# Transposes of x in 64-row halves among the query projections, the early weight bits in new places, and the first key exponential ahead of the denominator

## The chip, the core and the metric

The kernel runs on one core of one Trainium2 chip. The metric is the device time of one execution in microseconds (us), as the median of several runs. TensorE (PE) multiplies matrices and also does the transposes; VectorE (DVE), ScalarE (ACT) and GpSimd (POOL) do elementwise work, and SyncE (SP) issues the DMA transfers. Each engine works through its own instructions in program order, and engines wait for one another through semaphores.

## The reference, cut to what matters

```python
def phi(x):
    proj = np.einsum('bhsd,df->bhsf', x, w_phi)
    proj = proj - np.max(np.abs(proj), axis=-1, keepdims=True)
    return np.concatenate([np.exp(proj), np.exp(-proj)], axis=-1)
q_p, k_p = phi(q), phi(k)             # 8 batches, 8 heads, 576 tokens, 64 -> 2*128
kv  = np.einsum('bhsf,bhsd->bhfd', k_p, v)
z   = np.sum(k_p, axis=2)
num = np.einsum('bhsf,bhfd->bhsd', q_p, kv)
den = np.einsum('bhsf,bhf->bhs', q_p, z)[..., None] + 1e-06
x   = (num / den).transpose(0, 2, 1, 3).reshape(4608, 512)
h   = x @ w_in                         # 512 -> 2048
g   = h * np.tanh(softplus(h))
out = g @ w_out                        # 2048 -> 512
```

## The kernel before, in words

The program has two stages on one core: the attention, up to about 270 us of the trace, and the feed-forward layer after it. The change is in the attention and in the weight preparation that runs beside it.

The attention is cut into 36 units of 512 rows (`NU`). For a unit of keys there are these steps, named by their functions. `k_proj` (L292 in `project`) multiplies 64-row slices of the keys by `w_phi` into a PSUM tile `pp_k`: eight matmuls, the two 64-row halves of the partitions in turn. `k_center` takes the maximum `m_k` (L300) and subtracts it into `e_k` (L301), both on DVE. `k_exp` takes the two exponentials on ACT (L345 and L346). `k_sum` multiplies by the values into `kvps` (L309), and `k_store` copies `kvps` to `kv` on ACT (L371).

For a unit of queries: `q_proj` into `pp_q` (L292), `q_center` into `m_q` and `e_q` on DVE, `q_turn` transposes `e_q` into two tiles `dt` (L396; sixteen transposes of 64 rows), `q_exp` takes four exponentials of `dt` on ACT (L401), and `q_num` multiplies by `kv` into `num` (L309, two tiles). `q_den` copies the denominators from `num` to `r` on ACT (L421); `q_norm` takes the reciprocal and multiplies into `x` on DVE (L426, L429). A unit later `q_out` transposes x on PE into one tile `xt` (L438, four transposes of 128 rows), and `q_store` copies it to `xs` on ACT (L445) and sends it to `x_spill` by DMA (L446). In a middle unit PE runs in the order `dt`, `pp_k`, `xt`, `pp_q`, `num`, `kvps`, each step for another unit of rows.

PSUM tiles come from two pools. `ps_a` has two buffers, which `pp_k` and `pp_q` take in turn, so every `pp_q` of the middle units has the same buffer as the `pp_q` before it. `ps_b` has four buffers, shared by `dt`, `xt`, `num` and `kvps`. A tile's first write waits for the last reader of the tile that held the buffer before.

Beside this, `weight_ops` prepares 16 of the weight pieces in the attention (`EARLY`), one in about two units: `absolute` on ACT (L183), `clamp` (L186), `shift` (L190), `sign` (L194) and `scale` (L200) on DVE, then `low_scale` (L209), multiplications and sums on POOL, a cast on ACT (L243) and a subtraction on POOL (L247).

Near the end of the attention, `x_load` (L462) brings x back from DRAM and `x_block` casts it into blocks `xc` (L484), which go to `xc_spill` (L488).

The order on each engine is written out by hand: every step is registered with a planned time (`at(time, fn)`), the events are sorted by that time, and the sorted order is the program's order on each engine. The planned time has no other use; nothing waits for a clock. A unit is planned as 7.341 us (`STEP`), and `K_AT` and `Q_AT` are the offsets of its steps.

Of the kernel before, what the change touches and what calls it, by code (L numbers as in the profile page):

```python
# [8 lines left out]
F32 = mybir.dt.float32  # L9
# [7 lines left out]
P = 128  # L17
# [14 lines left out]
LEAD = 4  # L32
# [12 lines left out]
Q_AT = (1.52, 3.149, 6.11, 6.455, 1.875, 3.0, 6.564, 9.042)  # L45
T_AT = (0.95, 2.19, 4.9, 5.3, 8.55, 10.92, 12.6, 13.1)
JOIN = 0.99
JOIN_AT = ((-4.6, -4.5, -4.46, -3.7), (0.0, 0.9, 1.8, 2.8))
PRE = (11.72, 6.53)
CONV = (13.41, 14.719)  # L50
WORD_AT = 4.79
X0_AT = (38.06, 20.0)
X0_SUM_AT = 31.75
X0_BLOCK_AT = (26.35, 26.3, 22.18, 22.17, 22.16, 17.38, 17.33)
# [30 lines left out]
def attention_then_mish(ctx, tc, qT, kT, va, w_phi, w_in, w_out, w_out2, out):  # L85
# [80 lines left out]

    def weight_ops(kind, fp, k, quiet):

# [16 lines left out]
        def clamp():  # L185
            nc.vector.tensor_scalar(w(), w(), LARGE, SMALL, op0=ALU.min, op1=ALU.max)  # L186

# [23 lines left out]
        def low():  # L211
            if not quiet:
                low_scale()
            f, t = low_word(), piece[key][2]
            nc.gpsimd.tensor_tensor(t, f, t, op=ALU.mult)
# [54 lines left out]

        ops = [(0.0, absolute), (0.9, clamp), (1.35, shift), (1.8, sign), (2.5, scale)]
        if quiet:
            ops.insert(1, (0.2, low_scale))
# [8 lines left out]
    def project(raw, name, cuts=(0, 4)):  # L282

        parts = []
        for a, b in zip(cuts, cuts[1:]):
            ps = ps_a.tile([P, 2, 4, F], F32, tag="pp", name=f"pp_{name}_{a}")
# [6 lines left out]
        return parts  # L293

    def center(parts, name):
# [44 lines left out]

    def k_exp(n):
        e = k_live[n]
        for a, b in zip(cuts_of(n), cuts_of(n)[1:]):
            cols = slice(a * P, b * P)
            nc.scalar.activation(e[:, :, 1, cols], e[:, :, 0, cols], AF.Exp)  # L345
            nc.scalar.activation(e[:, :, 0, cols], e[:, :, 0, cols], AF.Exp, scale=-1.0)  # L346
# [33 lines left out]
    def q_proj(n):  # L380
        q_live[n] = project(q_live.pop(n), f"q_{n}")

    def q_center(n):
# [57 lines left out]
    def q_store(n):  # L441
        c, g = divmod(n, 2)
        ps = out_live.pop(n)
        xs = att.tile([P, 2, CH], F32, tag="xs", name=f"xs_{n}", bufs=2)
        nc.scalar.copy(xs, ps)  # L445
        nc.sync.dma_start(x_spill[c][:, 2 * g:2 * g + 2, :], xs)  # L446
# [30 lines left out]
    def x_block(s, b):  # L477
# [8 lines left out]
        xc[s].append(blk)  # L486
        if not seen_before[s] and s + 1 != seg2:
            nc.sync.dma_start(xc_spill[segs[s][0], b], blk.rearrange("p h k s -> p h (k s)").bitcast(F32))  # L488

# [290 lines left out]
    for u in range(NU):  # L780
# [5 lines left out]
        at(t + (LOAD_AT[1] if u > LEAD else V_AT[u]), v_load, u)  # L786
        at(t + a[0], k_proj, u)
        at(t + a[1], k_center, u)
        at(t + a[2], k_exp, u)
        at(after + a[3], k_sum, u)  # L790
# [9 lines left out]
        at(t + LOAD_AT[2] - early, q_load, u)  # L800
        at(t + a[0] - early, q_proj, u)
        at(t + a[1] - early, q_center, u)
# [6 lines left out]
        at(end + a[5] + 0.05, q_norm, u)  # L809
        at(close_by + a[6] + (1.78 if u in (NU - LEAD - 2, NU - LEAD - 1) else 0.0), q_out, u)  # L810
        at(close_by + a[7] + (0.9 if u == NU - 1 else 0.0), q_store, u)

# [33 lines left out]
    for i, pc in enumerate(pieces):  # L846
# [5 lines left out]
        else:  # L852
            clock = CONV[0] + CONV[1] * i - WORD_AT
            load_at = clock + WORD_AT + (LOAD_AT[3] if i else -12.0)
        at(load_at, weight_load, *pc)
        bits, sums, high, spill = weight_ops(*pc, quiet)
        for delay, op in bits:
            wait = base(2 * i + 1) + Q_AT[1] + 0.02 if i < 2 and delay else 0.0
            at(max(clock + delay * (0.85 if quiet else 1.0), wait - (0.49 if i == 0 else 0.0)), op)
        clock += LOW_AT[which] if quiet else WORD_AT  # L860
        for j, (cost, op) in enumerate(sums):
            at(clock, op)
            if pc[1] >= 2 and j in (high, len(sums) - 1):
                at(clock + SPILL_AT[j > high and not quiet], spill, int(j > high))
            clock += cost
            if i == EARLY - 1 and sums[j + 1:j + 2] and j + 1 == high:
                clock += 1.2

    for s, (sc, fps) in enumerate(segs):
# [10 lines left out]
        for i in range(4):  # L880
            at((begin - X0_SUM_AT if s == 0 else t_of(n - 2) + X_SUM_AT if late_sums else t + XS_AT[1] + (XS2 if s == 3 else 0.0)) + XS_AT[2] * i, x_sum, s, i)
        for b in range(7):
            if n >= AHEAD + 2:
# [144 lines left out]
```

## Time and profile before

| | us |
|---|---|
| median of 3 runs | 1017.37 (1017.09 to 1017.58) |
| profiled execution, its own time | 1015.56 |
| its span in the trace | 1013.7 |
| PE busy | 1004.0 (99%) |
| DVE busy | 759.9 (75%) |
| ACT busy | 505.1 (50%) |
| POOL busy | 277.2 (27%) |

The span runs from the first to the last recorded instruction; 1.86 us of the profiled execution lie outside it. The granted clock of TensorE was 1.0, the higher level of 2.4 GHz, in every stretch of the attention that is shown below. A row of a timeline gives the start and the length of one instruction, or of several of one kind, and, in brackets, how long the engine stood idle before it and what ended that. Matmuls are pipelined, so that the start of the next step tells more than the length of one. The records of one fp32 matmul are two, so x16 stands for eight matmuls.

### The profile page before, as it was taken

The page shows a single profiled execution, that of the slowest core. Times are in us where ns is not written, and L with a number is a line of the kernel's source. Part 1 is how long each engine was busy: PE and PEld are TensorE (multiplying, and loading weights), DVE is VectorE, ACT ScalarE, POOL GpSimd, SP SyncE. Part 2 cuts the span into 40 slices and gives each one's busy share as a digit, 9 for nine tenths or more (in the row PEclk, how much of TensorE's full clock was granted, in tenths as well). Part 3 has the DMA queues.
Part 4 walks back from the last instruction along what each step waited for, and adds up shares of the span by engine and source line. Part 5 has one row for each costly group of instructions (what it writes and reads, how often), then busy time and mean ns, then how long its engine had stood idle before and what let it go on. Part 6 is the DMA issues. An engine that isn't in the chain of part 4 may idle for free.

```text
span 1013.7 us, 28698 instructions
## 1 busy us (share of the span) xinstructions
PE 1004.0 (99%) x12298; PEld 956.9 (94%) x12298; DVE 759.9 (75%) x1184; ACT 505.1 (50%) x874; POOL 277.2 (27%) x251
## 2 busy tenths in 40 slices
PE   8999999999999999999999999999999999999998
PEld 7899999999899999999999999999999999999998
DVE  6899999999657788878985675757575757575755
ACT  5778777877754445554453433333333333333332
POOL 0454435545515244466436010101010101010101
PEclk9999999999999999999999999999999999999999
DMA  7556567776887869898858995858586858686841
GB/s 222 173 186 182 183 207 255 252 243 196 278 303 297 324 253 325 271 330 303 281 200 298 344 360 209 324 209 321 210 320 217 313 218 312 219 311 222 308 167 73
DMA packets 111199, 259.00 MB, mean 256 GB/s; under 512 B 8672, under 2 KB 47328, under 8 KB 109024
## 3 DMA queue, kind: packets, MB, share of 16 engines
q1 hardware_dynamic: 111072, 257.17, 71.9%
q8 instruction: 97, 1.59, 0.6%
q14 instruction: 30, 0.25, 0.1%
HBM read 179.27 MB, written 77.86 MB: 254 GB/s over the span
## 4 chain that ended last, share of the span: by engine, by line
PE 96%; ACT 2%; DVE 1%; DMA 1%; issue 0%; DVEq 0%; ACTq 0%
PE h L519 36%; PE o L671 22%; PE o L648 15%; PE num L309 6%; PE kvps L309 6%; PE pp_k L292 3%; PE pp_q L292 3%; PE dt L396 2%; PE xt L438 2%; ACT e_q L401 1%; DMA x_spill<-xs 1%; DVE e_k L301 0%; DVE m_k L300 0%; DMA head<-w_phi 0%; ACT e_k L345 0%
## 5 line engine op out<-in xcount | busy, mean ns | idle before, releaser
L519 PE MATMUL h<-xc,win 128*128 128x256 f32 x3024 | 380.4, 283 | 0.0
L519 PEld LDWEIGHTS h<-xc,win 128*128 128x128 f32 x3024 | 373.8, 192 | 4.5
L743 POOL TENSOR_TENSOR part<-part,du 128x512 f32<-128x512 f32 x18 | 23.3, 1297 | 425.7 <-DVE du L733 425.7
L671 PE MATMUL o<-wa,gh 128*128 128x256 f32 x720 | 130.7, 283 | 0.0
L671 PEld LDWEIGHTS o<-wa,gh 128*128 128x128 f32 x720 | 111.8, 192 | 0.0
L648 PE MATMUL o<-wout,gh 128*128 128x512 f32 x432 | 108.2, 392 | 0.0
L551 DVE TENSOR_TENSOR u<-h,u 128x512 f32<-128x512 f32 x72 | 49.4, 687 | 70.4 <-PE h L519 70.4
L671 PE MATMUL o<-wa,gl 128*128 128x256 f32 x360 | 100.7, 283 | 0.0
L671 PE MATMUL o<-wb,held 128*128 128x256 f32 x795 | 95.8, 281 | 0.2 <-DVE du L733 0.2
L671 PEld LDWEIGHTS o<-wb,held 128*128 128x128 f32 x795 | 94.9, 189 | 0.4 <-DVE du L733 0.4
L648 PEld LDWEIGHTS o<-wout,gh 128*128 128x128 f32 x432 | 77.7, 189 | 13.9
L309 PE MATMUL num<-kv,e_q 128*64 128x65 f32 x2304 | 78.5, 223 | 1.3 <-ACT e_q L401 0.8
L309 PEld LDWEIGHTS num<-kv,e_q 128*64 128x64 f32 x2304 | 72.2, 137 | 7.1 <-ACT e_q L401 2.3
L567 ACT ACTIVATE sb<-h 128x256 f32<-128x256 f32 x45 | 17.3, 385 | 120.0 <-PE h L519 85.8
L309 PE MATMUL kvps<-v,e_k 128*64 128x65 f32 (+1 forms) x2560 | 76.8, 222 | 0.0
L401 ACT ACTIVATE e_q<-dt 128x512 f32<-128x512 f32 x144 | 74.2, 604 | 4.3 <-PE dt L396 3.7
L570 ACT ACTIVATE u<-u 128x768 f32<-128x768 f32 x45 | 38.1, 846 | 72.8 <-DVE u L551 72.8
L309 PEld LDWEIGHTS kvps<-v,e_k 128*64 128x64 f32 (+1 forms) x2560 | 72.5, 137 | 1.7 <-issue 0.2
L606 ACT CAST gh<-sb 128x1024 fp32r<-128x1024 f32 x45 | 47.2, 1050 | 50.0 <-DVE sb L599 50.0
L671 PEld LDWEIGHTS o<-wa,gl 128*128 128x128 f32 x360 | 68.6, 192 | 0.0
L618 DVE TENSOR_TENSOR gl<-sb,gh 128x1024 fp32r<-128x1024 f32 x45 | 61.0, 1356 | 0.7 <-ACT gh L606 0.7
L648 PE MATMUL o<-wout,gl 128*128 128x512 f32 x216 | 57.7, 389 | 0.0
(101 smaller groups left out, 1592.2 us busy)
## 6 DMA issues: line engine op xcount, KB each, us to landing
win<-in_spill SPq DMA_DIRECT2D x44, 896.0 KB, 8.0
xc<-xc_spill SPq DMA_DIRECT2D x63, 512.0 KB, 5.8
xc_spill<-xc SPq DMA_DIRECT2D x56, 512.0 KB, 6.0
wa<-out_spill SPq DMA_DIRECT2D x29, 768.0 KB, 5.7
in_spill<-wst_in SPq DMA_DIRECT2D x24, 448.0 KB, 2.7
v<-va SPq DMA_DIRECT2D x32, 325.0 KB, 3.9
qraw<-qT SPq DMA_DIRECT2D x36, 256.0 KB, 3.7
x_spill<-xs SPq DMA_DIRECT2D x36, 256.0 KB, 2.9
```

Of the source, the lines that this page charges most:

```text
L292: nc.tensor.matmul(ps[:, j, n], src, w_phi2[rows], start=True, stop=True)
L309: nc.tensor.matmul(ps[rows], lhsT[:, rows], rhs[h], start=start, stop=stop, skip_group_check=True)
L396: nc.tensor.transpose(turned[n, h][:, jj, i], e[rows, jj, 0, i * P:(i + 1) * P], ident[rows, rows])
L401: nc.scalar.activation(e[:, s, h], ps, AF.Exp, scale=2.0 * s - 1.0)
L519: nc.tensor.matmul(ps, w, x, start=(i in (0, 2) and m == 0), stop=(m == 5), skip_group_check=True)
L551: nc.vector.tensor_tensor(u[:, 0:3:2] if second(n) else u[:, 1:3], hy, u2.unsqueeze(1).broadcast_to([P, 2, CH]), op=ALU.add)
L570: nc.scalar.activation(u[:, 0:3], u[:, 0:3], AF.Mish)
L606: nc.scalar.copy(gh, u_live[n][4])
L618: nc.vector.tensor_tensor(gl, u_live[n][4], g_live[n]["h"].bitcast(F32), op=ALU.subtract)
L648: nc.tensor.matmul(o_live[s][tt], g[:, 2 * f + which, cols], wout[fp][:, f, k], start=(first and g is gh and f == k == 0), stop=(last and ...
L671: nc.tensor.matmul(ps, g, w, start=(start and k == 0), stop=(stop and k == 2), skip_group_check=True)
L743: nc.gpsimd.tensor_tensor(cross, cross, d_live[s, tau][0].unsqueeze(1).broadcast_to([P, 2, CH]), op=ALU.add)
```

## The change

It has these parts.

- x's transposes. For units 3 to 32 of the queries, the new `q_proj_out` writes the eight projections of the unit and, among them, the transposes of x of the unit three before, as eight transposes of 64 rows into two tiles `xt0` and `xt1`. `q_store` copies the two tiles to `xs` in two instructions. Units 30 to 35 of x keep `q_out`.
- The early weight bits of pieces 2 to 15. The clamp goes from DVE to POOL. `absolute` and `clamp` stand one unit earlier; `shift` and `sign` stand on DVE between the keys' centring and the reciprocal; `scale` follows a unit later, again behind the keys' centring. `low_scale` is a step of its own.
- The first of a key unit's two exponentials goes ahead of the two `r` on ACT, the second stays behind them.
- The two parts of the projection of key unit 0 share one PSUM tile, `k_proj` of unit 5 comes 1.7 planned us earlier, the stores of the first seven `xc` blocks are steps of their own (`block_store`), and one `q_store` is 0.68 earlier.

```diff
+EXP_AT = 2.95
+BEAT_AT = (-5.73, -5.54, 1.9, 1.91, 9.24, 7.84)
+BEAT_LOW, BEAT_HI = 9.34, 16.43
+X0_STORE_AT = (16.4, 16.35, 16.3, 16.25, 16.2, 15.0, 14.9)
...
         def clamp():
-            nc.vector.tensor_scalar(w(), w(), LARGE, SMALL, op0=ALU.min, op1=ALU.max)
+            (nc.vector if quiet else nc.gpsimd).tensor_scalar(w(), w(), LARGE, SMALL, op0=ALU.min, op1=ALU.max)
...
         ops = [(0.0, absolute), (0.9, clamp), (1.35, shift), (1.8, sign), (2.5, scale)]
+        if early:
+            ops = list(zip(BEAT_AT, (absolute, clamp, shift, sign, scale, low_scale)))
+        elif not quiet:
+            ops = [(0.0, absolute), (0.6, clamp), (1.95, shift), (2.25, sign), (2.7, scale)]
...
+    def project_turn(raw, name, x, ps_x):
+
+        ps = ps_a.tile([P, 2, 4, F], F32, tag="pp", name=f"pp_{name}")
+
+        def proj(j, n):
+            rows = slice(j * D, (j + 1) * D)
+            nc.tensor.matmul(ps[:, j, n], raw[rows, n * P:(n + 1) * P], w_phi2[rows], start=True, stop=True)
+
+        def turn(h):
+            rows = slice(h * D, (h + 1) * D)
+            for i in range(2):
+                for t in range(2):
+                    nc.tensor.transpose(ps_x[h][:, i, t], x[rows, i, t], ident[rows, rows])
+
+        proj(1, 0)
+        turn(0)
+        for n in range(4):
+            proj(0, n)
+            if n < 3:
+                proj(1, n + 1)
+        turn(1)
+        return [(0, 4, ps)]
...
-    def k_exp(n):
+    def k_exp(n, s):
+        e = k_live[n]
+        nc.scalar.activation(e[:, :, s], e[:, :, 0], AF.Exp, scale=2.0 * s - 1.0)
...
+    def q_proj_out(n, m):
+        ps = [ps_b.tile([P, 2, 2, D], F32, tag="b", name=f"xt{h}_{m}") for h in range(2)]
+        q_live[n] = project_turn(q_live.pop(n), f"q_{n}", x_live.pop(m), ps)
+        out_live[m] = ps
...
-        nc.scalar.copy(xs, ps)
+        if isinstance(ps, list):
+            halves_of = xs.rearrange("p i (t h d) -> p h i t d", t=2, h=2)
+            for h in range(2):
+                nc.scalar.copy(halves_of[:, h], ps[h])
+        else:
+            nc.scalar.copy(xs, ps)
...
-        at(t + a[2], k_exp, u)
+        if u < LEAD:
+            at(t + a[2], k_exps, u)
+        else:
+            at(t + EXP_AT, k_exp, u, 1)
+            at(t + a[2], k_exp, u, 0)
...
-        at(t + a[0] - early, q_proj, u)
+        if 3 <= u <= NU - LEAD:
+            at(t + a[0], q_proj_out, u, u - 3)
+        else:
+            at(t + a[0] - early, q_proj, u)
```

On PE, in a middle unit of before, the four whole transposes of x (`xt`) stand between the projections of the keys and of the queries; `dt` is the transposed `e_q`.

```order
L396 MATMUL dt_16_2960<-ident,e_q_2799 128x64
L292 MATMUL pp_k_0_2977<-head,kraw_2805 128x128 x8
L438 MATMUL xt_2992<-ident,x_2864 128x128 x4
L292 MATMUL pp_q_0_3002<-head,qraw_2810 128x128 x8
L309 MATMUL num_16_3015<-kv_2062,e_q_2799 64x65 x8
```

In the same place after the change, the transposes are two blocks of four, one of each 64-row half, within the projections of the queries.

```order
L436 MATMUL dt_16_3061<-ident,e_q_2891 128x64
L300 MATMUL pp_k_3078<-head,kraw_2896 128x128 x8
L309 MATMUL pp_q_3095<-head,qraw_2900 128x128
L315 MATMUL xt_15_3093<-ident,x_2962 128x64 x4
L309 MATMUL pp_q_3095<-head,qraw_2900 128x128 x7
L315 MATMUL xt_15_3094<-ident,x_2962 128x64 x4
L340 MATMUL num_16_3120<-kv_2122,e_q_2891 64x65 x8
```

So `pp_q` now comes straight behind `pp_k`, and the last block of transposes straight ahead of `num`.

On DVE, one unit of before with weight work has the clamp and the shift ahead of the reciprocal of `r`, and the sign and the scale (`t_in`) behind the queries' centring (`m_q`, `e_q`).

```order
L300 TENSOR_REDUCE m_k_2900<-pp_k_0_2830 128x8
L301 TENSOR_TENSOR e_k_2899<-pp_k_0_2830,m_k_2900 128x2x512
L186 TENSOR_SCALAR w_in_0_2859<-w_in_0_2859 128x512
L190 TENSOR_SCALAR w_in_0_2859<-w_in_0_2859 128x512
L426 RECIPROCAL r_2905<-r_2905 128x8
L429 TENSOR_TENSOR x_2864<-num_15_2865,r_2905 128x256
L429 TENSOR_TENSOR x_2864<-num_15_2866,r_2905 128x256
L300 TENSOR_REDUCE m_q_2945<-pp_q_0_2850 128x8
L301 TENSOR_TENSOR e_q_2944<-pp_q_0_2850,m_q_2945 128x2x512
L194 SCALAR_TENSOR_TENSOR w_in_0_2859<-words_in_0_2697,w_in_0_2859 128x512
L200 TENSOR_SCALAR t_in_0_2953<-w_in_0_2859 128x512
```

After the change the shift and the sign stand there, the scale follows in the next unit, and nothing stands between `e_q` and the next unit's `m_k`.

```order
L331 TENSOR_REDUCE m_k_3155<-pp_k_3078 128x8
L332 TENSOR_TENSOR e_k_3154<-pp_k_3078,m_k_3155 128x2x512
L194 TENSOR_SCALAR w_in_1_2955<-w_in_1_2955 128x512
L198 SCALAR_TENSOR_TENSOR w_in_1_2955<-words_in_1_2842,w_in_1_2955 128x512
L466 RECIPROCAL r_3164<-r_3164 128x8
L469 TENSOR_TENSOR x_3119<-num_16_3120,r_3164 128x256
L469 TENSOR_TENSOR x_3119<-num_16_3121,r_3164 128x256
L331 TENSOR_REDUCE m_q_3212<-pp_q_3095 128x8
L332 TENSOR_TENSOR e_q_3211<-pp_q_3095,m_q_3212 128x2x512
L331 TENSOR_REDUCE m_k_3319<-pp_k_3241 128x8
L332 TENSOR_TENSOR e_k_3318<-pp_k_3241,m_k_3319 128x2x512
L204 TENSOR_SCALAR t_in_1_3322<-w_in_1_2955 128x512
```

On ACT after the change, a unit with a cast of weights has the two half copies of x, the cast and the first key exponential ahead of the two `r`; before, the order there was one copy, the two `r`, and both exponentials.

```order
L441 ACTIVATE e_q_2891<-dt_16_3061 128x2x4x64 x2
L488 COPY xs_3112<-xt_15_3093 128x4x64
L488 COPY xs_3112<-xt_15_3094 128x4x64
L247 CAST wst_in_0_3116<-w_in_0_2643 128x896
L374 ACTIVATE e_k_3154<-e_k_3154 128x2x512
L461 ACTIVATE r_3164<-num_16_3120 128x4
L461 ACTIVATE r_3164<-num_16_3121 128x4
```

The two `r` have thus moved behind a key exponential and, in such a unit, behind the cast.

## Rows read from the trace of the kernel before

**Rows 1.** Page, its head and part 1: busy time of the engines, share, instructions.

```profile
span 1013.7 us, 28698 instructions
...
PE 1004.0 (99%) x12298; PEld 956.9 (94%) x12298; DVE 759.9 (75%) x1184; ACT 505.1 (50%) x874; POOL 277.2 (27%) x251
```

**Rows 2.** Busy time by stretch: first units, 25 middle units, tail of the attention.

```profile
core 0: us, PE busy (x) PEld busy (x) DVE busy (x) ACT busy (x) POOL busy (x), PEclk, DMA share, GB/s
16.05:58.31 42.26, 41.17 (x1045) 37.77 (x1041) 37.55 (x47) 31.84 (x57) 17.48 (x17) 1.00 0.62 189
58.31:239.38 181.07, 181.07 (x4677) 168.34 (x4676) 166.79 (x226) 142.77 (x272) 84.65 (x79) 1.00 0.66 215
239.38:272.00 32.62, 31.32 (x741) 28.49 (x741) 24.66 (x38) 25.69 (x59) 19.88 (x16) 1.00 0.74 237
```

**Rows 3.** Timeline of PE in a middle unit.

```profile
157.57 0.71 PE L396 MATMUL dt<-ident,e_q 64*128 64x64 f32 x16
158.12 1.11 PE L292 MATMUL pp_k<-head,kraw 64*128 64x128 f32 x16
159.16 0.66 PE L438 MATMUL xt<-ident,x 128*128 128x128 f32 x4
159.74 1.16 PE L292 MATMUL pp_q<-head,qraw 64*128 64x128 f32 x16
160.83 2.09 PE L309 MATMUL num<-kv,e_q 128*64 128x65 f32 x64
```

**Rows 4.** Timeline of DVE in that unit.

```profile
158.25 1.23 DVE L301 TENSOR_TENSOR e_q<-pp_q,m_q 128x1024 f32<-128x1024 f32 x1
159.39 0.68 DVE L194 SCALAR_TENSOR_TENSOR w_in<-words_in,w_in 128x512 uint32<-128x512 uint32 x1
...
161.77 1.23 DVE L301 TENSOR_TENSOR e_k<-pp_k,m_k 128x1024 f32<-128x1024 f32 x1
163.17 0.20 DVE L426 RECIPROCAL r<-r 128x8 f32<-128x8 f32 x1 [0.18 <-ACT r L421]
...
165.40 1.22 DVE L301 TENSOR_TENSOR e_q<-pp_q,m_q 128x1024 f32<-128x1024 f32 x1
```

**Rows 5.** Timelines of DVE and PE early on, where `pp_q` waited for `e_q`.

```profile
49.21 1.22 DVE L301 TENSOR_TENSOR e_q<-pp_q,m_q 128x1024 f32<-128x1024 f32 x1
...
50.49 0.71 PE L292 MATMUL pp_q<-head,qraw 64*128 64x128 f32 x8
```

**Rows 6.** Timeline of PE, 0.04 us where `num` begins behind `pp_q`.

```profile
240.27 0.28 PE L292 MATMUL pp_q<-head,qraw 64*128 64x128 f32 x2
240.47 0.28 PE L309 MATMUL num<-kv,e_q 128*64 128x65 f32 x2
```

**Rows 7.** Timeline of ACT in the unit of rows 3.

```profile
158.35 2.07 ACT L401 ACTIVATE e_q<-dt 128x512 f32<-128x512 f32 x4
160.27 0.62 ACT L445 COPY xs<-xt 128x512 f32<-128x512 f32 x1
...
162.97 0.17 ACT L421 ACTIVATE r<-num 128x4 f32<-128x4 f32 x1 [0.29 <-PE num L309]
163.04 1.05 ACT L345 ACTIVATE e_k<-e_k 128x1024 f32<-128x1024 f32 x1
...
165.08 0.36 ACT L371 COPY kv<-kvps 128x260 f32<-128x260 f32 x1
165.34 0.94 ACT L243 CAST wst_in<-w_in 128x896 fp32r<-128x896 f32 x1
```

**Rows 8.** Shift on DVE (L190), by shape, 16 to 239 us.

```profile
L190 DVE TENSOR_SCALAR w_in<-w_in x8: 426/844/846, 27.7 to 184.0; 128x512 uint32<-128x512 uint32 x8
```

**Rows 9.** Timeline of DVE, the first units.

```profile
22.30 1.23 DVE L300 TENSOR_REDUCE m_k<-pp_k 128x8 f32<-128x1024 f32 x1 [1.08 <-PE pp_k L292]
```

**Rows 10.** Timeline of PE, the attention's tail.

```profile
255.41 2.09 PE L309 MATMUL num<-kv,e_q 128*64 128x65 f32 x64 [0.29 <-ACT e_q L401]
...
269.46 0.71 PE L396 MATMUL dt<-ident,e_q 64*128 64x64 f32 x15 [0.36 <-ACT xs L445]
```

More of the change, by code (lines that the diff above doesn't have):

```diff
@@ L165, in weight_load, with weight_ops @@
         piece[kind, fp, k] = [words.rearrange("p (a b) -> p b a", b=2)]
-    def weight_ops(kind, fp, k, quiet):
+    def weight_ops(kind, fp, k, quiet, early):
         key = (kind, fp, k)
@@ L211, in low @@
         def low():
-            if not quiet:
+            if not early and not quiet:
                 low_scale()
@@ L284, in project @@
         parts = []
+        ps = ps_a.tile([P, 2, 4, F], F32, tag="pp", name=f"pp_{name}")
         for a, b in zip(cuts, cuts[1:]):
-            ps = ps_a.tile([P, 2, 4, F], F32, tag="pp", name=f"pp_{name}_{a}")
             parts.append((a, b, ps))
@@ L293, in project @@
         return parts
+    def project_turn(raw, name, x, ps_x):
+        ps = ps_a.tile([P, 2, 4, F], F32, tag="pp", name=f"pp_{name}")
+        def proj(j, n):
[14 more added lines that the diff above has]
+        return [(0, 4, ps)]
     def center(parts, name):
@@ L339, in k_center, with k_exps @@
         k_live[n] = center(k_live.pop(n), f"k_{n}")
-    def k_exp(n):
+    def k_exp(n, s):
+        e = k_live[n]
+        nc.scalar.activation(e[:, :, s], e[:, :, 0], AF.Exp, scale=2.0 * s - 1.0)
+    def k_exps(n):
         e = k_live[n]
@@ L486, in x_block, with block_store @@
         xc[s].append(blk)
-        if not seen_before[s] and s + 1 != seg2:
-            nc.sync.dma_start(xc_spill[segs[s][0], b], blk.rearrange("p h k s -> p h (k s)").bitcast(F32))
+        if s and not seen_before[s] and s + 1 != seg2:
+            block_store(s, b)
+    def block_store(s, b):
+        nc.sync.dma_start(xc_spill[segs[s][0], b], xc[s][b].rearrange("p h k s -> p h (k s)").bitcast(F32))
     def x_back(s, b):
@@ L786, in attention_then_mish @@
         at(t + (LOAD_AT[1] if u > LEAD else V_AT[u]), v_load, u)
-        at(t + a[0], k_proj, u)
+        at(t + a[0] - (1.7 if u == LEAD + 1 else 0.0), k_proj, u)
         at(t + a[1], k_center, u)
-        at(t + a[2], k_exp, u)
+        if u < LEAD:
[3 more added lines that the diff above has]
+            at(t + a[2], k_exp, u, 0)
         at(after + a[3], k_sum, u)
@@ L809, in attention_then_mish @@
         at(end + a[5] + 0.05, q_norm, u)
-        at(close_by + a[6] + (1.78 if u in (NU - LEAD - 2, NU - LEAD - 1) else 0.0), q_out, u)
-        at(close_by + a[7] + (0.9 if u == NU - 1 else 0.0), q_store, u)
+        if u > NU - LEAD - 3:
+            at(close_by + a[6] + (1.78 if u in (NU - LEAD - 2, NU - LEAD - 1) else 0.0), q_out, u)
+        at(close_by + a[7] + (0.9 if u == NU - 1 else -0.68 if u == NU - LEAD - 2 else 0.0), q_store, u)
     begin = base(NU + 2) + JOIN
@@ L854, in attention_then_mish @@
             load_at = clock + WORD_AT + (LOAD_AT[3] if i else -12.0)
+        beat = 2 <= i < EARLY
+        bits, sums, high, spill = weight_ops(*pc, quiet, beat)
+        if beat:
+            clock = base(2 * i)
+            load_at = clock + BEAT_AT[0] - 6.0
         at(load_at, weight_load, *pc)
-        bits, sums, high, spill = weight_ops(*pc, quiet)
         for delay, op in bits:
-            wait = base(2 * i + 1) + Q_AT[1] + 0.02 if i < 2 and delay else 0.0
+            wait = base(2 * i + 1) + Q_AT[1] + 0.02 if i < 2 and delay > 1.0 else 0.0
             at(max(clock + delay * (0.85 if quiet else 1.0), wait - (0.49 if i == 0 else 0.0)), op)
-        clock += LOW_AT[which] if quiet else WORD_AT
+        clock += LOW_AT[which] if quiet else BEAT_LOW if beat else WORD_AT
         for j, (cost, op) in enumerate(sums):
+            if beat:
+                clock = base(2 * i) + (BEAT_HI + 0.1 * (j - high) if j >= high else BEAT_LOW + 0.1 * j)
             at(clock, op)
             if pc[1] >= 2 and j in (high, len(sums) - 1):
-                at(clock + SPILL_AT[j > high and not quiet], spill, int(j > high))
+                at(clock + (SPILL_AT[j > high and not quiet] if not beat else 1.2 if j == high else 3.2), spill, int(j > high))
             clock += cost
-            if i == EARLY - 1 and sums[j + 1:j + 2] and j + 1 == high:
-                clock += 1.2
     for s, (sc, fps) in enumerate(segs):
@@ L882, in attention_then_mish @@
         for b in range(7):
+            if s == 0:
+                at(begin - X0_STORE_AT[b], block_store, s, b)
             if n >= AHEAD + 2:
```

## The prediction, made before the changed kernel was run

> **What bounds the kernel now.** I read the page's head first. PE is busy for 1004.0 of 1013.7 us [rows 1], so what counts is what PE does and waits for. The table by stretch comes next: in the 25 middle units PE is busy for 181.07 of 181.07 us, 7.243 us a unit, while DVE is at 166.79 [rows 2]. By that view alone the middle is bound by PE, and each microsecond taken from PE there would be won. The timelines of PE and DVE, laid beside each other over one unit, say something else, and my forecast rests on that.
>
> Follow the buffer of `pp_q`. DVE ends `e_q` at 159.48 (158.25 + 1.23). The next `pp_q` takes the same PSUM buffer, so it can't start earlier; it starts at 159.74. `num` starts at 160.83, the reciprocal of its denominators at 163.17, and the next `e_q`, behind that reciprocal, the two products and `m_q` on DVE, ends at 166.62 (165.40 + 1.22) [rows 3, 4]. The steps are 0.26, 1.09, 2.34 and 3.45 us, together 7.14: a ring that closes once per unit. Three of the four are work or waits of fixed order. Only the first, 0.26, holds slack: where `pp_q` truly waited for `e_q`, it began 0.06 us after its end (49.21 + 1.22 to 50.49) [rows 5]. I take 0.08 for that hand-over. The ring's floor is thus 0.08 + 1.09 + 2.34 + 3.45 = 6.96 us, against 7.243 by PE. PE binds, but with only 0.28 us to spare before the ring does.
>
> **The transposes of x (units 3 to 32).** On PE, `pp_k` to `num` takes 2.71 us now (158.12 to 160.83) [rows 3], with the four whole transposes in between: 0.58 us of it from `xt` to `pp_q`. Without them, `pp_q` follows `pp_k` at the same shape after about 0.95 us (1.04 from `pp_k` to `xt`, less some 0.1, since the last pair needs 0.20 before another shape [rows 6] and only 0.11 before its own).
>
> Let X be the time from the start of `pp_q` to `num`. It is 1.09 now, and has the eight 64-row transposes in it afterwards. As a pair (one on each half of the partitions) a 64-row transpose costs little: the sixteen of `dt`, eight pairs, take 0.55 us from their start to `pp_k` (157.57 to 158.12 [rows 3]), 0.07 a pair, and 0.06 where the longer first step is left out. If each half of the array works through its own instructions, each half has four projections and four transposes, and X = 1.09 + 4 x 0.065 = 1.35. I take 1.36. If the halves wait for each other in program order, the four transposes at either end run alone: 1.09 + 8 x 0.065 = 1.61, and up to 1.85 where the projections lose their pairing too. So X lies between 1.34 and 1.85. For the lower end speaks that the records of a pair begin together: within 0.04 us two records of `num` begin, and the last two of `pp_q` share one start [rows 6].
>
> The Trainium skill, in "TensorE: Matmul & The Clock Gate" (Part 3, "What overlaps and what doesn't"), says that matmuls are strictly first in, first out, by start and by end. By that rule X would be at its upper end; the paired records [rows 6] allow both readings, since the two of a pair also stand one behind the other in the program.
>
> With X = 1.36 the two candidates for the unit are: PE, 7.243 - (2.71 - 0.95 - 1.36) = 6.84 us; the ring, 0.08 + 1.36 + 2.34 + 3.45 = 7.23 us. So PE gets 0.4 us shorter and the ring 0.27 us longer, and the ring takes over almost exactly where PE was. Steady gain: 25 x (7.23 - 7.243) = -0.3 us; PE would show waits of about 0.4 us a unit for `e_q`.
>
> **The copies and the first exponential.** The copy of `xs` becomes two of 128x256; one is near the 0.36 us of the 128x260 copy, so 0.72 instead of 0.62 [rows 7], on an engine with 38 us free in the middle [rows 2]. `num` now takes buffers of `dt1` and `xt0`, so it waits for the last `e_q` exponential (over at 160.42, 0.41 ahead of `num` [rows 3, 7]) and, for its second tile, for the first half copy; both have room, unless the `absolute` of a weight piece stands before them.
>
> The first key exponential ahead of `r` needs `e_k`, which ends 2.5 us (two passes of 1.23 [rows 4]) after `e_q`; it is 1.05 long and the next instruction starts 1.0 after it [rows 7], so `r` can go at about 3.5. `num` is through 0.08 + 1.36 + 2.1 = 3.54 after `e_q` [rows 3]. That just fits, and is costed at nothing. In the eight units with a 128x896 cast (`blocks` in `weight_ops` makes eight of the fourteen pieces such) the cast's 0.94 [rows 7] stands ahead of the exponential, behind the copies; the exponential then starts some 0.1 late, and so does `r`: 8 x 0.1 = +0.8 us. From below nothing, from above 0.3 in each of the 25: +7.
>
> **The weight bits on DVE.** The clamp leaves DVE for POOL, which has 96 us free in the middle [rows 2]. Shift and sign lie between `e_k` and the reciprocal: from 2.5 on, 0.43 to 0.85 for the shift [rows 8] and 0.68 for the sign [rows 4], to 3.6 to 4.0 us, where the reciprocal is due at 3.78 (0.08 + 1.36 + 2.34). At 0.43 it hides, and at 0.85 it costs 0.2 in fourteen units, 3 us. The median of the shift on w_in is 0.84 now [rows 8], but before, the clamp, the shift and POOL's `low_scale` ran at the same time, which the new places part; I take the short one, 0, and keep 3 for the range. What this buys is the other side of `e_q`: the sign and the scale no longer hold up `m_k` (from 159.48 to 160.5 in [rows 4]), without which the ring's 3.5 us for `m_k`, `e_k` and the bits would not fit.
>
> **First units and tail.** Before 58.31 us PE is idle for 1.09 of 42.26 us [rows 2], and DVE waits 1.08 us for `pp_k` at 22.30 [rows 9]. The projection of unit 5 comes earlier there, and the clamps leave: between 0 and -1.2, and I take half, -0.6. In the tail PE is idle for 1.30 us of 32.62 [rows 2]. Waits for the last exponentials and for copies of `xs`, up to 0.36 us each, are among it [rows 10]; the one at 269.46 is on a copy whose buffer was held by a store queued behind three `xc` stores on SP. Those stores are later now, and the transposes of the last units but three are gone from there. I take -0.5, with 0 and -1.0 as the ends. The loads behind the `xc` stores on SP have over ten us before the feed-forward layer asks for them, at 0.
>
> **Sum.** -0.3 + 0.8 - 0.6 - 0.5 = -0.6 us. The profiled execution would go from 1015.56 to 1015.0 us. It lies 1.81 below the median of the runs shown; on the median I forecast 1017.37 - 0.6 = 1016.8 us. Within 0.2% of the median (2.03 us) a change cannot be told from none for this kernel, so the forecast is "no change". Its own range is 1013.9 (tail and first units at their best, -2.2; X at 1.34 and the hand-over at 0.06, another 25 x 0.04 = -1.0; casts free) to 1020.9 (first units and tail at 0, the shifts at 0.85, +3).
>
> **Rivals.** First, slower: the halves run in program order at the two ends of the block. X is 1.60 to 1.85, the ring 7.47 to 7.72, and the 25 units cost 5.7 to 11.9 us, with the first units and the tail as above: 1022 to 1028 us. It decides from X = 1.46 on, where 25 units lose 2.5 us. For it speaks that the trace of before has no step in which one half of the array runs a block of its own while the other goes on, so that nothing there excludes it; against it, the paired records [rows 6]. Chance 0.11.
>
> Second, faster: the ring isn't closed, since some part of the 3.45 or 2.34 us was itself waiting for PE. Then PE alone binds at 6.84 and 25 units give 10 us: about 1006. For it speaks that PE shows no idle time in the middle [rows 2]; against it, that DVE has work back to back from the reciprocal to `e_q`, and that the reciprocal had waited for `r` [rows 4]. A half of it, 5 us, is as likely as all. Chance 0.13.
>
> Third, slower: the denominators come late in nearly every unit, since `r` stands behind a key exponential and a cast, and the reciprocal behind two bit operations. 0.15 to 0.3 us a unit, 25 units: +4 to +7, so 1020 to 1024. For it speaks the fit of 3.5 against 3.54 above, with no slack; against it, that a late `r` needs a late `e_k`, which now starts right behind `e_q`. Chance 0.13, of which 0.02 ends within 0.2%.
>
> **How the numbers follow.** The forecast has 0.63: 0.24 faster, 0.34 the same, 0.05 slower. With the rivals: faster 0.24 + 0.13 = 0.37; same 0.34 + 0.02 = 0.36; slower 0.05 + 0.11 + 0.11 = 0.27. The range 1012.0 to 1022.0 leaves out most of the first rival (0.10) and the better half of the second (0.07), and little else.
>
> **What would show it.** Right: in the middle stretch of the changed kernel PE is idle for about 0.3 to 0.4 us a unit ahead of `pp_q`, released by `e_q`; X reads 1.34 to 1.38; a unit takes 7.2 to 7.3 us; the reciprocal waits for `r` by less than 0.2. An X over 1.5 shows the first rival; a unit under 7.1 without waits on PE the second; an `r` that starts on ACT's queue and not on the end of `num`, with the reciprocal waiting for it in every unit, the third. Wrong altogether would be a difference that lies behind 272 us, in the feed-forward layer, which I hold unchanged.

## The result and the profile after

The changed kernel took 1023.62 us (median of six runs, 1021.09 to 1024.17), the kernel before 1017.19 us beside it: a ratio of 1.0062, with a 95% interval of 1.0052 to 1.0072. The forecast was 1016.8, the range ended at 1022.0: slower, where no change was forecast, and outside the range. The profiled execution took 1021.92 us, its span 1020.1, 6.4 longer than before.

The table by stretch says where. Columns as in [rows 2]; the bounds are the same `pp_q` of the program.

```profile
16.37:58.77 42.40, 39.49 (x1053) 36.80 (x1049) 37.03 (x46) 32.15 (x61) 24.10 (x27) 1.00 0.61 201
58.77:246.57 187.80, 175.82 (x4777) 165.59 (x4777) 166.70 (x214) 145.00 (x298) 97.34 (x88) 1.00 0.63 207
```

The 25 middle units take 187.80 us in place of 181.07 [rows 2], 6.73 more, and TensorE, busy for all of them before, now is idle for 12 us. The first units lose 0.14, the way from the last of these `pp_q` to the feed-forward layer's first matmul wins 1.03 (29.69 us in place of 30.72), and the start and the feed-forward layer lose 0.3 and 0.2.

Read from `pp_q` to `pp_q`, the 25 units fall into kinds. The four parts are those of the ring in the prediction: `e_q`'s end to `pp_q`, `pp_q` to `num`, `num` to the reciprocal, the reciprocal to `e_q`'s end. One unit of the shortest kind, DVE and then PE:

```profile
139.39 1.22 DVE L332 TENSOR_TENSOR e_q<-pp_q,m_q 128x1024 f32<-128x1024 f32 x1
...
144.35 0.20 DVE L466 RECIPROCAL r<-r 128x8 f32<-128x8 f32 x1 [1.01 <-ACT r L461]
...
146.57 1.22 DVE L332 TENSOR_TENSOR e_q<-pp_q,m_q 128x1024 f32<-128x1024 f32 x1
```

```profile
140.66 0.37 PE L309 MATMUL pp_q<-head,qraw 64*128 64x128 f32 x1 [0.67 <-DVE e_q L332]
...
142.01 2.09 PE L340 MATMUL num<-kv,e_q 128*64 128x65 f32 x64
...
147.85 0.37 PE L309 MATMUL pp_q<-head,qraw 64*128 64x128 f32 x1 [0.30 <-DVE e_q L332]
```

All 25:

```
units      length        ring: hand-over + X + num..reciprocal + reciprocal..e_q    over 7.19, sum
10         7.19          0.05 + 1.34 + 2.34 + 3.45                                  0
 6         7.32 to 7.35  0.05 + 1.34 + 2.47..2.50 + 3.45                            0.87
 6         7.78 to 7.84  0.05 + 1.34 + 2.94..3.01 + 3.45                            3.82
 1         8.84          0.06 + 1.34 + 4.00 + 3.44                                  1.65
 2         7.97, 8.12    0.06 + 1.35 + 3.11, 3.27 + 3.45                            1.71
```

25 x 7.19 + 8.05 = 187.80. Three of the four parts move by 0.02 at most. All that the long units take over 7.19 us lies between `num` and the reciprocal, and there it has three causes, one for each kind.

**The sign waits for POOL (7.8 and 8.8 us).** Timelines of DVE and then POOL in such a unit of the changed kernel; `num` had begun at 119.20.

```profile
116.58 1.23 DVE L332 TENSOR_TENSOR e_q<-pp_q,m_q 128x1024 f32<-128x1024 f32 x1
...
119.03 1.22 DVE L332 TENSOR_TENSOR e_k<-pp_k,m_k 128x1024 f32<-128x1024 f32 x1
120.17 0.42 DVE L194 TENSOR_SCALAR w_out<-w_out 128x512 uint32<-128x512 uint32 x1
120.62 1.66 DVE L198 SCALAR_TENSOR_TENSOR w_out<-words_out,w_out 128x512 uint32<-128x512 uint32 x1
122.20 0.19 DVE L466 RECIPROCAL r<-r 128x8 f32<-128x8 f32 x1
```

```profile
120.34 1.39 POOL L256 TENSOR_TENSOR w_out<-w_out,wout 128x512 f32<-128x512 f32 x1 [5.56 <-ACT wout L247]
```

The sign (L198) took 0.68 before [rows 4] and takes 1.66 here. POOL's subtraction ends at 121.73, and the sign 0.55 later. In the 8.84 us unit POOL's instruction is the wide one, of 2.10 us, and the sign takes 2.64, again to 0.55 after POOL's end. So the sign does not run at a lower rate, it stands until POOL is through. Rows of that unit, DVE and POOL:

```profile
165.92 2.64 DVE L198 SCALAR_TENSOR_TENSOR w_in<-words_in,w_in 128x512 uint32<-128x512 uint32 x1
168.48 0.19 DVE L466 RECIPROCAL r<-r 128x8 f32<-128x8 f32 x1
```

```profile
165.91 2.10 POOL L251 TENSOR_TENSOR wst_in<-w_in,wst_in 128x896 fp32r<-128x896 f32 x1 [3.09 <-ACT wst_in L247]
```

The bracket tells why they meet: the subtraction waits for ScalarE's cast, which the change has put into the same unit as shift and sign.

**Late words (7.97 and 8.12 us).** ACT and PE where a weight piece's words had not landed:

```profile
156.77 0.68 ACT L187 ACTIVATE w_in<-words_in 128x512 f32<-128x512 f32 x1 [0.69 <-DMA words_in<-w_in]
157.35 0.63 ACT L488 COPY xs<-xt 128x256 f32<-128x256 f32 x2
```

```profile
156.52 0.69 PE L340 MATMUL num<-kv,e_q 128*64 128x65 f32 x16
157.76 1.62 PE L340 MATMUL num<-kv,e_q 128*64 128x65 f32 x48 [0.55 <-ACT xs L488]
```

The copies of `xs` stand behind the absolute value, and the second tile of `num` needs the buffer that they empty.

**The cast ahead of the denominators (7.32 to 7.35 us).** Cast, exponential and `r` in a row on ACT, and what the reciprocal on DVE waited for:

```profile
149.60 0.94 ACT L247 CAST wst_in<-w_in 128x896 fp32r<-128x896 f32 x1
150.44 1.06 ACT L374 ACTIVATE e_k<-e_k 128x1024 f32<-128x1024 f32 x1
151.40 0.23 ACT L461 ACTIVATE r<-num 128x4 f32<-128x4 f32 x2
```

```profile
151.66 0.20 DVE L466 RECIPROCAL r<-r 128x8 f32<-128x8 f32 x1 [0.41 <-ACT r L461]
```

### The profile page after: what moved, and what is told of

It reads as the page before. It is cut to its first block, busy times and chain, and to the rows that moved or that the text cites. A ratio compares the mean times of both kernels' runs of the same rounds, so it can differ in the third digit from the quotient of the medians.

```text
span 1020.1 us, 28992 instructions
## 1 busy us (share of the span) xinstructions
PE 996.5 (98%) x12418; PEld 952.9 (93%) x12418; DVE 758.6 (74%) x1168; ACT 506.7 (50%) x904; POOL 290.2 (28%) x267
## 3 DMA queue, kind: packets, MB, share of 16 engines
q8 instruction: 98, 1.61, 0.6%
## 4 chain that ended last, share of the span: by engine, by line
PE 78%; DVE 14%; ACT 4%; DMA 2%; issue 2%; POOL 0%; SPq 0%; DVEq 0%; ACTq 0%
PE h L567 35%; PE o L719 22%; PE o L696 15%; DVE e_q L332 3%; DVE m_q L331 3%; PE num L340 2%; DVE m_k L331 2%; DVE x L469 2%; PE kvps L340 2%; ACT e_k L374 1%; DVE e_k L332 1%; PE pp_q L309 1%; DVE w_out L198 1%; PE pp_k L300 1%; DMA xc<-xc_spill 1%
## 5 line engine op out<-in xcount | busy, mean ns | idle before, releaser
L374 ACT ACTIVATE e_k<-e_k 128x1024 f32<-128x1024 f32 x64 | 67.6, 1056 | 11.0 <-DVE e_k L332 10.8
```

The costliest lines, as they stand in the source:

```text
L374: nc.scalar.activation(e[:, :, s], e[:, :, 0], AF.Exp, scale=2.0 * s - 1.0)
```

## The experiments

Theory A is this account: the ring through VectorE now binds at 7.19 us, and the sign, the words and the cast come on top. Theory B: the transposes among the projections are the loss themselves. C: it is ScalarE's new order. Ratios are to the kernel before, run on the same chip, with 95% intervals. Middle stretches are 25 units of the one profiled execution, which lies up to 3.6 us from its kernel's median.

**Cast and subtraction later.**

```diff
-BEAT_LOW, BEAT_HI = 9.34, 16.43
+BEAT_LOW, BEAT_HI = 9.34, 18.98
```

> The changed kernel with one number altered: the cast of an early weight piece and POOL's subtraction behind it come 2.55 planned us later, behind the reciprocal instead of beside shift and sign. Theory A (in the changed kernel VectorE's sign waits for a two-operand POOL instruction that runs at the same time: six units lose 0.65 and one 1.65 us, and six units lose 0.15 to the cast ahead of the denominators): every sign takes about 0.69 us in the middle units, those units fall from 7.84 and 8.84 to 7.2 to 7.35, the 25 middle units gain 5 to 6 us, and the time is 1017 to 1018.5 us. The cast now stands ahead of the query exponentials, which may give 1 us back. Rival B (the units are long because the ring through VectorE is, with the transposes in it, whatever POOL does): no change beyond 1 us, 1022.5 to 1024. Rival C (it is the cast on ScalarE ahead of the denominators): the sign stays at 1.66 where it is so now, and the gain is under 1.5 us.

1020.9 us, ratio 1.0039 (1.0024 to 1.0054); middle 184.77. All thirteen signs of the middle took 0.69, and the first five units took 7.19. But four units took 8.1 to 8.3, three of them behind a wide cast and one behind a narrow one: ScalarE does the cast ahead of the query exponentials there, everything behind them is late, and the second tile of `num` waits for `xs`. In the fourth, and in two more of 7.63 and 7.70, the absolute value waits for POOL besides (0.43 to 0.77 us). ACT and then PE in one of the three:

```profile
155.86 0.94 ACT L247 CAST wst_in<-w_in 128x896 fp32r<-128x896 f32 x1
156.71 2.06 ACT L441 ACTIVATE e_q<-dt 128x512 f32<-128x512 f32 x4
```

```profile
160.00 1.62 PE L340 MATMUL num<-kv,e_q 128*64 128x65 f32 x48 [0.49 <-ACT xs L488]
```

The mechanism held and the time missed: I put 1 us on the cast's new place, and it cost four units 0.9 to 1.1 each; the middle lies 5.0 us over 25 x 7.19 with no sign stalled.

**Words earlier.**

```diff
-            load_at = clock + BEAT_AT[0] - 6.0
+            load_at = clock + BEAT_AT[0] - 10.0
```

> The changed kernel with the loads of the early weight words 4 planned us earlier. Theory A: in two of the 25 middle units the absolute value on ScalarE waited for its words, the copies of xs and with them the second num tile came late (0.55 and 0.71 us of idle TensorE, 0.78 and 0.93 us longer units); these two waits go and the time falls by 1.7 us, to about 1022. Rival (the words come late because the DMA engines are full there, so an earlier issue is as late, or takes the place of keys and queries): no change, or other units lose as much, 1023 to 1025.

1021.66 us, 1.0045 (1.0032 to 1.0058), 1.7 below the changed kernel by the ratios, as expected, though the intervals overlap. Both late units are at 7.19; the profiled execution, the fastest of the eight at 1018.03, also has no sign of 2.64, its longest being 1.66. Middle 184.52.

**The halves alone.** The kernel before with `project_turn`, `q_proj_out`, the two half copies and the one earlier `q_store`, nothing else of the change.

> The kernel before with the transposes in halves among the query projections and the two half copies of xs, and nothing else of the change: clamp and shift stand ahead of the reciprocal, sign and scale behind the query centring, both key exponentials behind the denominators. Theory A (the halves alone only swap a TensorE bound of 7.24 us for a ring of 7.19, and the loss comes from the weight bits): 25 units take 7.19 to 7.35 each, the middle stretch 181 to 183 us, the time is 1015.5 to 1019. Rival B (the halves are the loss): 1021 to 1025.

1021.72 us, 1.0049 (1.0033 to 1.0066); middle 184.59. That is B's number, but not B's mechanism: twelve units are at 7.19. The six long ones (7.73 to 7.83) are those in which a wide weight cast stands ahead of the query exponentials, as it did before the change, too:

```profile
153.43 0.94 ACT L243 CAST wst_in<-w_in 128x896 fp32r<-128x896 f32 x1
154.27 2.06 ACT L429 ACTIVATE e_q<-dt 128x512 f32<-128x512 f32 x4
```

```profile
156.38 2.44 PE L332 MATMUL num<-kv,e_q 128*64 128x65 f32 x64 [0.20 <-ACT e_q L429]
```

`num` waits for the exponentials there (X 1.55 to 1.61), and in five of the six `r` comes later still, since `num` itself is drawn out by the late half copies (2.44 us in place of 2.09). So the halves do cost when they come alone: they use up the room in which the old order of the weight work was free. That I had not forecast for this run.

**The halves at the old place, in pairs.** The kernel before with eight 64-row transposes, the two halves in turn, between `pp_k` and `pp_q`, and the two half copies.

```diff
+                    for h in range(2):
+                        rows = slice(h * D, (h + 1) * D)
+                        nc.tensor.transpose(ps[h][:, i, t], x[rows, i, t], ident[rows, rows])
...
```

> The kernel before with x's transposes as eight of 64 rows in pairs, at the old place between the projections of keys and queries, and two half copies of xs; nothing else is changed. Theory A: TensorE has the same work as with the change, but from the start of the query projections to num it is 1.09 us again and not 1.34, so the ring's floor is 0.05 + 1.09 + 2.34 + 3.45 = 6.93 us and TensorE's own sum about 6.84; units take 6.93 to 7.15 and 25 of them gain 3 to 7 us on before: 1010.5 to 1014.5. What may hold it back is VectorE's bit work ahead of the reciprocal and query exponentials late behind a cast. Rival B (the ring is no ring, TensorE's own length alone counts): as fast as its sum, under 1009. Rival C (halved transposes cost on TensorE or in PSUM buffers what they save): 1016 to 1020.

1021.92 us, 1.0052 (1.0036 to 1.0069), rival C. Most units without a wide cast take 7.13 to 7.30, as before: the second `xt` takes the buffer of the first `dt` and waits for its exponentials in 22 of the 25, so TensorE's saving turns into a wait:

```profile
98.04 0.46 PE L469 MATMUL xt<-ident,x 64*128 64x64 f32 x7 [0.21 <-ACT e_q L429]
98.28 1.17 PE L292 MATMUL pp_q<-head,qraw 64*128 64x128 f32 x16
...
157.92 0.46 PE L469 MATMUL xt<-ident,x 64*128 64x64 f32 x7 [0.74 <-ACT e_q L429]
```

The loss comes where a wide cast stands ahead of those exponentials: the wait is 0.73 to 1.08 us there, and the seven units with one take 7.82 to 8.40.

**The rest of the change, without the halves.** `q_out` for all units again.

> The change without the transposes in halves: x is transposed whole, between the projections, as before; weight bits, exponential and stores are as in the change. Theory A: the ring's floor is 6.96 us again and TensorE's 7.24 binds, so a sign of 1.66 us (0.65 over) costs only what is beyond 0.28 us of slack, 0.35 in six units, and 1.3 in the worst; late words cost some 0.5 each; the tail's gain of 1 us stays: 1016.5 to 1020. Rival D (the moved bits lose the same whatever the transposes do): 1022 to 1024.

1033.12 us, 1.0164 (1.0149 to 1.0179), worse than either theory allowed. In twelve units `num` to the reciprocal takes 3.78 to 4.35 us. DVE and POOL:

```profile
124.74 1.25 DVE L194 TENSOR_SCALAR w_out<-w_out 128x512 uint32<-128x512 uint32 x1
126.03 1.66 DVE L198 SCALAR_TENSOR_TENSOR w_out<-words_out,w_out 128x512 uint32<-128x512 uint32 x1
```

```profile
124.43 1.28 POOL L256 TENSOR_TENSOR w_out<-w_out,wout 128x512 f32<-128x512 f32 x1 [4.93 <-ACT wout L247]
125.79 1.34 POOL L260 TENSOR_TENSOR wout<-w_out,t_out 128x512 fp32r<-128x512 f32 x1
```

Here the shift meets the first POOL instruction and the sign the second; in the changed kernel the shift has begun before either. I had carried the stall's size over from another alignment. The size is set by who comes first, and a few tenths decide it. As to cause: the moved weight work loses 17 us where no transposes are in the ring, though in another alignment than the change has.

**POOL's subtraction held until the reciprocal.** The changed kernel; the cast keeps its place, and the subtraction (L251, L256) and what follows it on POOL stand behind the new copy, 1.37 planned us later.

```diff
         nc.vector.reciprocal(r, r)
+        if n in gates:
+            g = mid.tile([P, 8], F32, tag="gate", name=f"gate_{n}", bufs=2)
+            nc.gpsimd.tensor_copy(g, r.rearrange("p a b c -> p (a b c)"))
...
```

> The changed kernel with a small copy on POOL (128x8, of the reciprocals) put ahead of POOL's subtraction behind the cast, so that the subtraction starts only when the unit's reciprocal is through; the cast itself stays where the change has it. Theory A (the sign on VectorE stands still while POOL runs a two-operand instruction): all signs of the middle units take about 0.69 us, the units that took 7.84 and 8.84 fall to 7.19 to 7.35, and 25 units gain about 5 us: 1017.5 to 1019.5 us. If the subtraction holds up the next operation of VectorE in the same way (the products of x, or m_q and e_q), these get longer by what the sign got shorter and nothing is gained: that is rival B, 1022.5 to 1024.5.

1019.91 us, 1.0032 (1.0021 to 1.0043), 3 us under the changed kernel and below its interval. The signs by shape, changed kernel first (16 to 250 us), this one second (58 to 250):

```profile
L198 DVE SCALAR_TENSOR_TENSOR w_out<-words_out,w_out x8: 693/1657/1666, 76.1 to 242.0; 128x512 uint32<-128x512 uint32 x8
```

```profile
L198 DVE SCALAR_TENSOR_TENSOR w_out<-words_out,w_out x8: 691/691/693, 76.4 to 238.7; 128x512 uint32<-128x512 uint32 x8
```

Eight units in a row, which had alternated between 7.19 and 7.78 to 7.84, take 7.19 here, and nothing behind the reciprocal became longer: rival B is out. The middle is still 184.31, since late words cost as much again in this execution, and TensorE stood twice for some 0.6 us within `kvps`, which the profile puts down to issue.

**With the earlier words too.** Both edits.

> The same small copy, and the loads of the weight words 4 planned us earlier. Theory A: the two gains add up, since they lie in different units: 25 units at 7.19, with 0.15 more in the units with a wide cast, 180.7 us, and 1015.5 to 1018 us in all, level with the kernel before. Rival: one of the two had hidden the other, 1019 to 1022.

1017.85 us, 1.0011 (1.0002 to 1.002): the two gains add up.

**Both exponentials behind the denominators.** The changed kernel with

```diff
-EXP_AT = 2.95
+EXP_AT = 3.584
```

> The changed kernel with both key exponentials behind the denominators, as before the change. Theory A (the exponential ahead of the denominators costs only where a cast pushes it, 0.15 us in six units, and some more where late words push it): 0.9 to 1.7 us faster than the changed kernel, 1021.9 to 1022.8. Rival C (the exponential ahead of the denominators is the main loss, since the denominators are late in most units): the reciprocal comes 2.34 us after num in all units but the stalled ones, and 4 us or more are won, under 1020. It may also lose, if kvps waits for the later exponentials.

1023.17 us, 1.0073 (1.0056 to 1.0091): not to be told from the changed kernel by time, where I had expected 0.9 to 1.7 us less; the four runs lie between 1020.47 and 1026.23. In the profile, of the fastest of them, the reciprocal comes 2.34 after `num` in all six units that had been 0.15 late, and the stalls of the sign stay. So late denominators, C, are out as the main cause.

**All three together.**

> The small copy, the earlier words and both exponentials behind the denominators together, with the transposes in halves and the moved weight bits kept. Theory A: all 25 units near the ring's floor of 7.19 us, 179.8 to 180.5 us for them, 1014.5 to 1017 us: faster than the kernel before by 0 to 2 us, and not by more, since the ring and not TensorE sets the unit. Rival: TensorE's shorter sum (6.84 us a unit) shows through once the stalls are gone, under 1012.

1016.58 us, 1.0002 (0.9993 to 1.0011): level with the kernel before. Twenty of 25 units take 7.18 to 7.20, four 7.29 to 7.32; one takes 8.33, with 0.92 us of TensorE's in it that the profile puts down to issue. TensorE is busy for 174.63 us of the middle:

```profile
59.93:241.28 181.35, 174.63 (x4777) 165.04 (x4777) 159.74 (x214) 146.81 (x298) 92.72 (x101) 1.00 0.65 213
```

So the three fixes take the whole loss back, and TensorE's 6.7 idle us show that something else binds.

**Is it the ring?** First a small copy on DVE between the reciprocal and the products, in the kernel before and in the last one:

```diff
         nc.vector.reciprocal(r, r)
+        extra = mid.tile([P, 8], F32, tag="extra", name=f"extra_{n}", bufs=2)
+        nc.vector.tensor_copy(extra, r.rearrange("p a b c -> p (a b c)"))
```

> The kernel before with one more small copy (128x8) on VectorE between the reciprocal and the products of x, so that the way from the reciprocal to the end of e_q gets longer by d (0.2 to 0.3 us, to be read from the records). Theory A (before, the ring through VectorE has 0.2 to 0.35 us of slack in a unit, since TensorE's transposes stand between e_q's end and the next pp_q): the copy takes up the slack, units stay near 7.15 and 7.31, 25 of them lose 0 to 2 us; 1016.5 to 1019. Rival B (VectorE isn't on a closed path): no change in any unit. Rival C (VectorE sets the unit already): 25 x d, 5 to 7.5 us slower.

> The changed kernel with the three stalls taken out (small copy on POOL, earlier words, both exponentials behind the denominators), and the same extra copy on VectorE. Theory A (with the transposes among the query projections the ring is the bound and has no slack): every middle unit goes from 7.19 to 7.19 + d, 25 units and some at both ends lose 5 to 8 us, 1021.5 to 1024.5. Rival B (TensorE is the bound there too): under 2 us lost, 1016.5 to 1018.5.

1020.35 us (1.0037, 1.0023 to 1.0051) and 1019.18 us (1.003, 1.0019 to 1.004), neither within a range that was stated for it. Inconclusive: the copy takes 0.17 us of the 0.31 that pass between the reciprocal and the products anyway, so d was 0.01. What it cost, it cost where POOL was at work. DVE and POOL in the kernel before with the copy:

```profile
91.96 1.08 DVE L428 COPY extra<-r 128x8 f32<-128x8 f32 x1
92.95 0.74 DVE L431 TENSOR_TENSOR x<-num,r 128x256 f32<-128x256 f32 x2
```

```profile
91.73 1.28 POOL L256 TENSOR_TENSOR wout<-w_out,t_out 128x512 fp32r<-128x512 f32 x1
```

A copy of eight columns ends 0.03 us after POOL's instruction. Then the first product of x, which reads PSUM, was done twice:

```diff
-        for i in range(2):
-            ps = num_live.pop((n, i))
+        for i in (0, 0, 1):
+            ps = num_live[n, i]
```

> The kernel before with the first of the two products of x done twice on VectorE (it reads PSUM; the same values are written again), so that the way from the reciprocal to the end of e_q is longer by d, some 0.34 us, in every unit. The extra copy of the earlier run did not lengthen that way: it lay in the time between the reciprocal and the products that passes anyway. Theory A (before, the ring's floor is 0.05 + 1.09 + 2.34 + 3.45 = 6.93 us, TensorE takes 7.15 or 7.31): the floor becomes 7.27, units go to 7.27 to 7.31, and 25 of them lose about 1.5 us, with a little more at both ends: 1017.5 to 1019.5. Rival C (VectorE sets the unit already): 25 x 0.34 = 8.5 us lost, 1024 to 1026.

> The changed kernel with its three stalls taken out (small copy on POOL, earlier words, both exponentials behind the denominators) and the same doubled product. Theory A (with the transposes among the query projections the ring is the bound, with no slack): every middle unit goes from 7.19 to 7.53, 25 units lose 8.5 us and the time is 1024 to 1027. Rival B (TensorE is the bound in that kernel as well): under 2.5 us lost, 1016.5 to 1019.

1022.61 us (1.0058, 1.0041 to 1.0075) and 1027.78 us (1.0106, 1.0091 to 1.0121). The reciprocal to `e_q`'s end is 3.91 in both, so d was 0.46 and not 0.34, and both times lie above Theory A's ranges. The kernel before goes to 0.05 + 1.09 + 2.34 + 3.91 = 7.39: it now takes 7.39 or 7.40 in 17 of 25 units. The other goes to 7.65, 7.19 + 0.46, in 24 of 25. The middle stretches, before with the doubled product and then the other:

```profile
59.10:245.84 186.74, 184.10 (x4676) 169.61 (x4676) 175.69 (x251) 144.25 (x271) 84.84 (x79) 1.00 0.62 208
```

```profile
60.74:252.01 191.27, 174.75 (x4777) 165.48 (x4777) 169.68 (x239) 148.93 (x298) 92.55 (x100) 1.00 0.61 202
```

The same 0.46 costs the first 5.67 us in 25 units, half of 25 x 0.46, and the second 9.92 (11.5 less the 1.6 us by which the kernel without the product was over 25 x 7.19 in its execution). Before, there was slack for half of it; with the transposes in the ring there is none. By time, too: 0.58% against 1.04%. The ring is what binds.

## Why the prediction was wrong, step by step

**Right: the ring and its floor.** Hand-over 0.05 (taken as 0.08), X 1.34 (1.36), 2.34 and 3.45 as read; 7.19 (7.23) us a unit, reached in ten units, and in twenty once the stalls are out. TensorE's waits ahead of `pp_q` for `e_q` are there. The list of waits, of the weight loads and the matmuls:

```profile
PEld pp_q L309 <- DVE e_q L332: 17.2, 29, 1.1
PE pp_q L309 <- DVE e_q L332: 10.6, 21, 1.0
```

The second rival (TensorE's 6.84) fell with that, and the first (the halves in program order, X from 1.60) with X. In one block of the changed kernel:

```profile
156.17 0.22 PE L315 MATMUL xt<-ident,x 64*128 64x64 f32 x1
156.21 0.27 PE L309 MATMUL pp_q<-head,qraw 64*128 64x128 f32 x1
...
156.32 0.27 PE L309 MATMUL pp_q<-head,qraw 64*128 64x128 f32 x1
```

A transpose of the last block begins 0.04 us ahead of both records of the projection that stands before it in the program, and one begins ahead in 29 of the 30 units with such blocks: between the two row halves TensorE does not start in the program's order. The Trainium skill's strict order ("TensorE: Matmul & The Clock Gate", Part 3, "What overlaps and what doesn't") does not hold between two row halves in these records.

**Wrong: the weight bits on DVE.** The step was "At 0.43 it hides, and at 0.85 it costs 0.2 in fourteen units, 3 us ... I take the short one, 0". The sign was taken at 0.68 whatever POOL does. Measured: 3.82 + 1.65 = 5.5 us in the middle, seven signs of 1.66 and 2.64. Two things were wrong in it. The shift's 0.84 [rows 8] was taken as the most that POOL costs; it is a wait, whose length hangs on what is left of POOL's instruction, so 0.85 was no upper end. DVE and POOL before:

```profile
155.04 0.85 DVE L190 TENSOR_SCALAR w_in<-w_in 128x512 uint32<-128x512 uint32 x1
```

```profile
154.05 1.56 POOL L209 TENSOR_SCALAR w_in<-words_in 128x512 f32<-128x512 uint32 x1
```

The shift ends 0.28 us after POOL, as do the five others of that length; in the kernel before with the doubled product they begin up to 0.1 us later beside `low_scale`, take 0.72 to 0.79, and end the same 0.28 after it. And of what "the new places part", only POOL's `low_scale` was looked at. The cast is moved as well, and POOL's subtraction follows it into the very place of shift and sign. The Trainium skill has the rule ("SBUF — State Buffer", "Who interferes with whom"): a VectorE instruction with two inputs in SBUF and a GpSimd instruction that reads SBUF lock each other out for a whole instruction, and so do one in a two-port mode and any GpSimd instruction. The trace agrees for the sign, which has two SBUF inputs and stands beside POOL's subtraction; `m_k`, `e_k` and the products, which read PSUM, take their 1.22 and 0.76 us beside POOL. It does not agree beside `low_scale`: in four units of the run without the halves the sign took 1.02 to 1.04 there and ended 0.33 us ahead of POOL's instruction. No run shows in which mode the shift works.

**The third rival: the right place, and its time by luck.** It held the right place, the reciprocal, and 1023.62 lies in its 1020 to 1024. But it priced a small delay, 0.15 to 0.3 us, in nearly every unit, with `r` late. That part came to 0.87 us in six units, close to the +0.8 of the sum. The rest is few units with large waits.

**Missed: the late words, 1.71 us.** The loads of the words are moved too; I counted no cost for them. One stands on SP's queue behind a store of `wst_in`, which begins as the moved cast ends (149.60 + 0.94, above):

```profile
150.57 0.33 SPq L271 DMA_DIRECT2D in_spill<-wst_in  x1
151.00 1.42 SPq L168 DMA_DIRECT2D words_in<-w_in  x1
```

**First units and tail.** -0.6 was forecast for the first: +0.14. One unit there has five bit operations on DVE and takes 8.83 us, of which 3.99 lie between `num` and the reciprocal. The tail won 1.03, where I took 0.5 with 1.0 as the end.

With the sign's 5.5 and the words' 1.7 put in, the sum of -0.6 becomes +6.6; the medians differ by 6.4. That it fits so closely is in part luck, since smaller misses cancel: the steady gain was 25 x (7.19 - 7.243) = -1.3 and not -0.3, the first units +0.1 and not -0.6, the tail -1.0 and not -0.5, and the start and the feed-forward layer, at 0 in the sum, +0.5.

## What to carry to other kernels

An engine that is busy for 100% of a stretch may have a closed path through other engines a quarter of a microsecond behind it; follow a buffer from its release to its next release before pricing a saving. When a step is moved, list what runs on every other engine at its new place, and above all what the moved steps themselves release there. A duration with two values in the trace is a question (what ran beside it?) and its larger value is no bound.

## What the runs showed of the hardware

- Three DVE instructions that work in SBUF alone were held until a POOL instruction, begun before them, was through: 0.69 became 1.66 and 2.64 for the sign, 0.42 became 1.25 and up to 2.26 for the shift (run without the halves), 0.17 became up to 1.25 for a 128x8 copy in the middle units. They ended 0.55, 0.28 and 0.03 us after POOL; beside `low_scale` alone the sign got through earlier, at 1.02 to 1.04. The reciprocal, in SBUF as well, was not held (0.19 to 0.20 us each of the 32 times that it began beside POOL in the changed kernel), and neither were DVE instructions that read PSUM.
- The two 64-row halves of TensorE work through their own instructions: four transposes on one half and four projections beside them on the other add 0.25 us to X (1.09 to 1.34), as pairs would.
- A small operation that only copies a result may cost nothing on a chain of dependent instructions: 0.31 us pass between the reciprocal and its consumer, and the 0.17 us copy fits in.
